# Attention with mixed heads and a mixture of experts on one core: the ten queries of a half lie 12 partitions apart in the evicted scores

## Chip, cores and metric

The kernel runs on one core of a Trainium2 chip. The metric is the time of one execution on the device in microseconds (us), as the median of several runs.

## The reference

There are B = 8 batches, H = 12 heads, S = 448 tokens, 64 numbers a head. Cut to what matters:

```python
scores = (1 / 8) * q @ k.transpose(0, 1, 3, 2)          # b h i j
scores = einsum('bhij,hg->bgij', scores, w_pre)         # heads are mixed
attn = softmax(scores, over j)
attn = einsum('bhij,hg->bgij', attn, w_post)            # heads are mixed again
x = (attn @ v).transpose(0, 2, 1, 3).reshape(3584, 768)
# eight experts; each token goes to the one with the highest gate
e = argmax(x @ w_gate); g = softmax(x @ w_gate)[e]
out = g * (relu(x @ w1[e]) @ w2[e])
```

## The kernel before

**Tiles.** A batch's 448 queries are cut into four tiles of `IT` = 120, the last with 88. A tile is `T`, 32 in all; `it = T % 4`. A tile is worked through in blocks of up to 20 queries, a block in two halves of `IB` = 10: six blocks for 120 queries, five for 88 (the last block has one half of 8). There are 184 blocks and 360 halves. `geom[T]` holds the batch, `it`, the number of queries and the sizes of the halves by block.

**One tile.**
- `qk` (L205): for each of six head pairs, scores of 120 queries against 448 keys, in three matmul passes of split numbers; two heads go to PSUM `bs`. ScalarE evicts them to `SI[T]` (L207): the partition is the query, and a partition holds all 12 heads, 12 x 448 floats side by side. There are two `si` buffers, so a tile's first eviction has to wait until the relayouts of the tile two before have read theirs.
- `relayout` (L224): one DMA on SyncE's queue for each half moves ten partitions of `SI[T]` to 120 partitions of `sb`, one for each query and head. A packet is one head's row of 1,792 bytes. `sb` has four buffers.
- `mix` (L234 to L236): a matmul with `Wpre`, which is block diagonal over queries, mixes the heads of a half into `bm`; VectorE takes the maxima (L235), ScalarE the exponential and its sum into `et` (L236).
- `weigh` (L244 to L249): reciprocals, and GpSimd scales `Wpost` with them into `wp`.
- `post` (L260): four matmuls for each half, with `et` as the stationary operand, mix the heads again and turn the rows: `bp` has keys on partitions, and (key chunk, head, query) along them. VectorE copies `bp` into `PT[T]` (L265), where the query is the last dimension.
- `av`, `rows`, `dispatch` (L280 to L345): attention times `v`, tokens and gates, and the routing table. `XD` takes the tokens.

The keys of the next batch come in by six loads `kr` (L88), which ScalarE and GpSimd split into `kh` and `kl` (L95, L96); queries by `qr` (L104), split at L113 and L114. Both loads are issued on SyncE's queue, among the relayouts.

**Order.** A table of steps says in which block each step of a tile is written: `qk` eight blocks ahead, `relayout` two blocks ahead, `post` one block behind `mix`. Each engine works in its own fixed order. SyncE issues the DMAs in that order as well; each waits for its buffer there.

**Experts.** From about 1060 us on, each expert's tokens are gathered and go through two weight matrices, again split. The weights come in by `wraw` (L359), the first of them during the last tiles of attention.

Of the kernel before, what the change touches and what calls it, by code (L numbers as in the profile page):

```python
# [19 lines left out]
B, H, S, D = 8, 12, 448, 64  # L20
# [5 lines left out]
IB = 10  # L26
NB = 2 * IB
IQ = 5
R0, R1 = 4, 124
# [11 lines left out]
def attn_moe_kernel(ctx, tc, qT, kT, v, w_pre, w_post, w_gate, w1, w2, out):  # L41
    nc = tc.nc
# [4 lines left out]
    XD = dram.tile([NT, HD], F32, name="XD")  # L47
    TB = dram.tile([ROWS, 2], F32, name="TB")

    geom = []  # L50
    for T in range(NTILE):
        it = T % 4
        ni = min(IT, S - it * IT)
        geom.append((T // 4, it, ni, [[min(IB, ni - i) for i in range(s, min(s + NB, ni), IB)]
                                      for s in range(0, ni, NB)]))


    kq = ctx.enter_context(ExitStack())
# [23 lines left out]
    KR, KK, QR, QQ, VV, SI, SB, EE, PT, XT = ({} for _ in range(10))  # L82
# [14 lines left out]
        KK[b, c] = (kh, kl)  # L97

    def load_q(T):
        b, it, ni, _ = geom[T]  # L100
        qr = q_p.tile([P, NPAIR, IT], F32, name="qr", bufs=1)
        src = qT[b, :, H * it * IT:H * (it * IT + ni)].rearrange("d (c t i) -> t d c i", c=NPAIR, t=2)
        for half in range(2):
            nc.sync.dma_start(out=qr[half * D:(half + 1) * D, :, :ni], in_=src[half])  # L104
        QR[T] = qr
# [26 lines left out]
    for c in range(NPAIR):  # L132
# [22 lines left out]
        out=Wpre[:, R0:].rearrange("p (i g) -> p i g", g=H),  # L155
# [13 lines left out]
    for c in range(NPAIR):  # L169
# [22 lines left out]
                        in_=none.unsqueeze(1).to_broadcast([P, 8, ROWS // P // 8, 2]))  # L192


    def qk(T, c):
        b, it, ni, _ = geom[T]
        if c == 0:
            SI[T] = si_p.tile([IT, H, S], F32, name="si")
        kh, kl = KK[b, c]
        qh, ql = QQ[T]  # L200

        for n, (qx, kx) in enumerate(((qh, kh), (qh, kl), (ql, kh))):
            for r in range(2):
                hs = slice(r * D, (r + 1) * D)
                nc.tensor.matmul(out=bank_s[:ni, r, :S], lhsT=qx[hs, c, :ni], rhs=kx[hs, :],  # L205
                                 start=(n == 0), stop=(n == 2))
        nc.scalar.copy(out=SI[T][:ni, 2 * c:2 * c + 2, :], in_=bank_s[:ni, :, :S])  # L207
        m = (it - 2) * NPAIR + c - NPAIR + 2
        if b + 1 < B:
            if 0 <= m < NPAIR:  # L210
                load_k(b + 1, m)
            if 1 <= m <= NPAIR:
                split_k(b + 1, m - 1)
# [5 lines left out]
    def relayout(T, s):  # L219
        sb = sbs[nsb["n"] % len(sbs)]  # L220
        nsb["n"] += 1
        for c, nq in enumerate(geom[T][3][s]):
            q0 = s * NB + c * IB
            nc.sync.dma_start(out=sb[R0:R0 + nq * H, c, :], in_=SI[T][q0:q0 + nq])  # L224
        SB[T, s] = sb

    def mix(T, s):
# [25 lines left out]
    def post(T, s):  # L253
        if s == 0:
            PT[T] = pt_p.tile([JC, NJ, H, IT], F32, name="pt")
        et, wp = EE.pop((T, s))
        for n, nq in enumerate(geom[T][3][s]):
            pp = bank_p[n]
            for c in range(NJ):
                nc.tensor.matmul(out=pp[:, c * IT:(c + 1) * IT],  # L260
                                 lhsT=et[:R1, n, c * JC:(c + 1) * JC],
                                 rhs=wp[:R1, n, :], start=True, stop=True)
        for n, nq in enumerate(geom[T][3][s]):
            i0 = s * NB + n * IB
            nc.vector.tensor_copy(  # L265
                out=PT[T][:, :, :, i0:i0 + nq].rearrange("p c h i -> p (c h) i"),
                in_=bank_p[n][:, :NJ * IT].rearrange("p (x i) -> p x i", i=IB)[:, :, :nq])

    PA = {}


    def av(T, g):
        b, it, ni, _ = geom[T]
        if g == 0:
            XT[T] = x_p.tile([P, NPAIR, IT], F32, name="xt")
        for p in range(3):
            for c in range(NJ):
                for r in range(2):
                    h = 2 * (3 * g + p) + r
                    nc.tensor.matmul(out=bank_a[r * D:(r + 1) * D, p, :ni],  # L280
                                     lhsT=VV[b][:, c, h * D:(h + 1) * D],
                                     rhs=PT[T][:, c, h, :ni], start=(c == 0), stop=(c == NJ - 1))
        nc.vector.tensor_copy(out=XT[T][:, 3 * g:3 * g + 3, :ni], in_=bank_a[:, :, :ni])  # L283
# [1 line left out]
    XR, LG = {}, {}  # L285

    def rows(T, part):
        b, it, ni, _ = geom[T]
        if part == 0:
            XR[T] = x_p.tile([IT, NPAIR, P], F32, name="xr", bufs=1)  # L290
            LG[T] = sm_p.tile([IT, 2, NE], F32, name="lg")
        px = bank_x[part] if T == NTILE - 1 else bank_x[0]
        pxv = px[:, :3 * XG].rearrange("p (c x) -> p c x", x=XG)
        for c in range(3):
            nc.tensor.matmul(out=pxv[:ni, c, :], lhsT=XT[T][:, part * 3 + c, :ni],
                             rhs=xg[:, part * 3 + c, :], start=True, stop=True)
        nc.scalar.copy(out=XR[T][:ni, part * 3:part * 3 + 3, :], in_=pxv[:ni, :, :P])
        nc.vector.reduce_sum(out=LG[T][:ni, part, :],
                             in_=pxv[:ni, :, P:XG].rearrange("p c e -> p e c"), axis=AX.X)
        if part == 1:  # L300
            t0 = b * S + it * IT
            nc.sync.dma_start(out=XD[t0:t0 + ni, :],
                              in_=XR.pop(T)[:ni].rearrange("p c x -> p (c x)"))
# [1 line left out]
    state = {"base": base0}  # L305

    def dispatch(T):
        b, it, ni, _ = geom[T]
        lg2 = LG.pop(T)
        lg = sm_p.tile([IT, NE], F32, name="lgs")  # L310
        nc.vector.tensor_add(out=lg[:ni], in0=lg2[:ni, 0, :], in1=lg2[:ni, 1, :])
        m8 = sm_p.tile([IT, NE], F32, name="m8")
        i8 = sm_p.tile([IT, NE], U32, name="i8")
        nc.vector.max(out=m8[:ni], in_=lg[:ni])
        nc.vector.max_index(out=i8[:ni], in_max=m8[:ni], in_values=lg[:ni])
        sc = sm_p.tile([IT, 4], F32, name="sc")
        nc.vector.tensor_copy(out=sc[:ni, 0:1], in_=i8[:ni, 0:1])
        ohb = sm_p.tile([IT, NE], BF16, name="ohb")
        nc.vector.tensor_scalar(out=ohb[:ni], in0=iota8[:ni], scalar1=sc[:ni, 0:1], scalar2=None,
                                op0=ALU.is_equal)  # L320
        pr = bank_x[0]
        nc.tensor.matmul(out=pr[:ni, 0:NE], lhsT=tri[:ni, :ni], rhs=ohb[:ni], start=True, stop=True)
        nc.tensor.matmul(out=pr[:, NE:2 * NE], lhsT=ones[:ni, :], rhs=ohb[:ni], start=True, stop=True)
        nc.vector.tensor_scalar(out=sc[:ni, 1:2], in0=m8[:ni, 0:1], scalar1=-1.0, scalar2=None,
                                op0=ALU.mult)
        ex = sm_p.tile([IT, NE], F32, name="ex")
        nc.scalar.activation(out=ex[:ni], in_=lg[:ni], func=AF.Exp, bias=sc[:ni, 1:2],
                             scale=1.0, accum_out=sc[:ni, 2:3])
        nc.vector.tensor_scalar(out=sc[:ni, 2:3], in0=sc[:ni, 2:3], scalar1=1e-9, scalar2=None,
                                op0=ALU.add)  # L330
        tg = sm_p.tile([IT, 2], F32, name="tg")
        nc.vector.reciprocal(out=tg[:ni, 1:2], in_=sc[:ni, 2:3])
        nc.vector.tensor_copy(out=tg[:ni, 0:1].bitcast(I32), in_=tokid[:ni, b, it:it + 1])
        pos = sm_p.tile([IT, NE], F32, name="pos")
        nc.vector.tensor_tensor(out=pos[:ni], in0=pr[:ni, 0:NE], in1=state["base"][:ni], op=ALU.add)
        nc.vector.tensor_tensor(out=pos[:ni], in0=pos[:ni], in1=ohb[:ni], op=ALU.mult)
        di = sm_p.tile([IT, 1], I32, name="di")
        nc.vector.reduce_sum(out=sc[:ni, 3:4], in_=pos[:ni], axis=AX.X)
        nc.vector.tensor_copy(out=di[:ni], in_=sc[:ni, 3:4])
        nc.gpsimd.indirect_dma_start(  # L340
            out=TB[:, :], out_offset=bass.IndirectOffsetOnAxis(ap=di[:ni, 0:1], axis=0),
            in_=tg[:ni, :], in_offset=None, bounds_check=ROWS - 1, oob_is_err=False)
        last = T == NTILE - 1
        nbase = (const if last else sm_p).tile([P, NE], F32, name="cbase" if last else "nbase")
        nc.vector.tensor_tensor(out=nbase, in0=pr[:, NE:2 * NE], in1=state["base"], op=ALU.add)  # L345
        state["base"] = nbase
# [31 lines left out]
        steps.setdefault(u, []).append(what)  # L378

    for T in range(NTILE):  # L380
        b, it, ni, _ = geom[T]
        u0, n = ustart[T], len(geom[T][3])
        if T:
            at(max(u0 - QLEAD - 4, -1), 0, load_q, T)
# [178 lines left out]
    with tc.For_i(0, nslots, 1):  # L563
# [20 lines left out]
        for n, rows in enumerate((HD, FF)):  # L584
# [9 lines left out]
            out=tb[:, :], out_offset=None, in_=TB[:, :],  # L594
# [74 lines left out]
```

## Time and profile before

| | |
|---|---|
| median of 3 runs | 1654.72 us (1654.67 to 1656.5) |
| the profiled execution | 1650.6 us |
| its span | 1648.4 us |
| mean granted clock of TensorE | 0.974 |
| DMA | 197.51 MB, mean 120 GB/s |

The profile is of one execution. PE is TensorE's matmul, PEld its weight load, DVE is VectorE, ACT ScalarE, POOL GpSimd, SP SyncE; SPq is SyncE's queue, where a row's length is the time that the issue took, not that of the transfer. In rows of groups, "out<-in" gives tile names, then the shapes (partitions x elements), the count, the busy time in us, the mean ns of one, and the idle time before it with what ended it. In square brackets of a timeline row stands the idle time of that engine just before, and what ended it.

### The profile page before, as it was taken

Reading aid. Unit: us, or ns where it says so; the run is one execution under the profiler, and the core shown is the slowest. Engines: PE = TensorE matmul, PEld = TensorE weight load, DVE = VectorE, ACT = ScalarE, POOL = GpSimd, SP = SyncE. Lnnn points to the kernel's source line nnn. Section 1 sums busy time; section 2 is a strip of 40 time slices with the busy share of each in tenths; the row PEclk is TensorE's granted clock in tenths of the full one; section 3 lists DMA queues with packets and bytes.
Section 4 is the critical chain, followed back from the end, with each engine's and each line's share of the span. In section 5 each row is a group of like instructions: output and inputs, shape, how many; then the busy total and the mean of one; then the engine's idle time right before and its main releaser. Section 6 shows DMA issues by size and latency. Waiting matters only on the chain. (4 is left out here: it accounts for less than half of the span.)

```text
span 1648.4 us, 29453 instructions
## 1 busy us (share of the span) xinstructions
PE 1528.3 (93%) x11056; PEld 1202.8 (73%) x11056; DVE 816.0 (50%) x2003; ACT 663.2 (40%) x1424; POOL 429.3 (26%) x595
## 2 busy tenths in 40 slices
PE   4798998998998998998999998859999999999996
PEld 2576776776776776776777776659888888997986
DVE  0465665564665565664666666643342433335330
ACT  3454444454454444444445443323241332224220
POOL 4243243243233333333333321222020210102000
PEclk9899999999999999999999999979999999999998
DMA  6555655565566565565555545253351624326210
GB/s 163 120 114 111 121 127 111 99 145 115 99 139 127 98 138 116 107 134 118 112 126 112 110 87 135 68 174 123 133 183 55 219 76 154 132 93 220 94 48 36
DMA packets 114465, 197.51 MB, mean 120 GB/s; under 512 B 39746, under 2 KB 88914, under 8 KB 114308
## 3 DMA queue, kind: packets, MB, share of 16 engines
q1 hardware_dynamic: 107200, 171.51, 44.7%
q0 software_dynamic: 6064, 23.86, 4.0%
q8 instruction: 100, 1.64, 0.4%
q14 instruction: 57, 0.47, 0.1%
q10 hardware_dynamic: 1044, 0.04, 0.0%
HBM read 96.01 MB, written 23.06 MB: 72 GB/s over the span
## 5 line engine op out<-in xcount | busy, mean ns | idle before, releaser
L236 ACT ACTIVATE et<-bm,st 124x448 f32<-124x448 f32 x360 | 226.2, 633 | 408.0 <-DVE st L235 325.6
L260 PEld LDWEIGHTS bp<-wp,et 124*112 124x112 f32 x2880 | 314.3, 179 | 70.2 <-issue 53.6
L249 POOL TENSOR_SCALAR wp<-Wpost,st 124x120 f32<-124x120 f32 x360 | 208.2, 590 | 602.5 <-DVE st L246 567.6
L260 PE MATMUL bp<-wp,et 124*112 124x120 f32 x2880 | 350.9, 275 | 13.7 <-POOL wp L249 8.8
L234 PE MATMUL bm<-sb,Wpre 124*124 124x448 f32 x720 | 307.9, 549 | 2.9 <-DMA sb<-si 2.9
L265 DVE COPY pt<-bp 112x480 f32<-112x480 f32 x360 | 234.3, 653 | 79.7 <-PE bp L260 78.0
L235 DVE TENSOR_REDUCE st<-bm 124x1 f32<-124x448 f32 x360 | 224.0, 623 | 47.2 <-PE bm L234 36.0
L207 ACT COPY si<-bs 120x896 f32<-120x896 f32 (+1 forms) x192 | 172.4, 898 | 66.8 <-PE bs L205 39.2
L280 PEld LDWEIGHTS ba<-pt,vt 112*64 112x64 f32 x3072 | 157.8, 141 | 33.3 <-issue 21.4
L280 PE MATMUL ba<-pt,vt 112*64 112x120 f32 (+1 forms) x3072 | 175.3, 269 | 1.2 <-DVE pt L265 0.7
L234 PEld LDWEIGHTS bm<-sb,Wpre 124*124 124x124 f32 x720 | 121.2, 189 | 73.1 <-issue 65.5
L205 PEld LDWEIGHTS bs<-kh,qh 64*120 64x120 f32 (+1 forms) x384 | 34.7, 177 | 165.3 <-issue 94.9
L525 POOL DMA_INDIRECT out<-y,ti x30 | 33.4, 1112 | 465.1 <-ACT xh L452 337.7
L497 PE MATMUL pm_h<-xh,ah 128*128 128x512 f32 (+1 forms) x384 | 147.3, 384 | 1.9 <-ACTq L549 0.8
L497 PE MATMUL pm_h<-xh,al 128*128 128x512 f32 (+1 forms) x384 | 146.9, 383 | 0.0
L497 PE MATMUL pm_h<-xl,ah 128*128 128x512 f32 (+1 forms) x384 | 146.9, 383 | 0.0
L205 PE MATMUL bs<-kh,qh 64*120 64x448 f32 (+1 forms) x384 | 92.2, 477 | 53.2 <-ACT si L207 44.4
L516 PE MATMUL pm_y<-bh,hh 128*128 128x384 f32 x480 | 127.9, 343 | 0.0
L516 PE MATMUL pm_y<-bl,hh 128*128 128x384 f32 x480 | 123.6, 336 | 0.0
L516 PE MATMUL pm_y<-bh,hl 128*128 128x384 f32 x480 | 121.0, 336 | 0.0
L501 DVE SCALAR_TENSOR_TENSOR hl<-pm_h,hh 128x512 fp32r<-128x512 f32 (+1 forms) x64 | 42.0, 657 | 139.1 <-ACT hh L500 139.1
L283 DVE COPY xt<-ba 128x360 f32<-128x360 f32 (+1 forms) x64 | 32.5, 507 | 139.0 <-PE ba L280 139.0
(102 smaller groups left out, 1746.4 us busy)
## 6 DMA issues: line engine op xcount, KB each, us to landing
sb<-si SPq DMA_DIRECT2D x352, 210.0 KB
wraw<-in_w SPq DMA_DIRECT2D x48, 512.0 KB
wraw<-in_w SPq DMA_DIRECT2D x64, 384.0 KB
kr<-in_kT SPq DMA_DIRECT2D x48, 224.0 KB
vt<-in_v SPq DMA_DIRECT2D x8, 1344.0 KB
qr<-in_qT SPq DMA_DIRECT2D x48, 180.0 KB
XD<-xr SPq DMA_DIRECT2D x24, 360.0 KB
qr<-in_qT SPq DMA_DIRECT2D x16, 132.0 KB
```

The source lines that it names most:

```text
L205: nc.tensor.matmul(out=bank_s[:ni, r, :S], lhsT=qx[hs, c, :ni], rhs=kx[hs, :], start=(n == 0), stop=(n == 2))
L207: nc.scalar.copy(out=SI[T][:ni, 2 * c:2 * c + 2, :], in_=bank_s[:ni, :, :S])
L234: nc.tensor.matmul(out=bm, lhsT=Wpre[:R1, :], rhs=sb[:R1, c, :], start=True, stop=True)
L235: nc.vector.reduce_max(out=st[:R1, 0, c:c + 1], in_=bm, axis=AX.X, negate=True)
L236: nc.scalar.activation(out=et[:R1, c, :], in_=bm, func=AF.Exp, bias=st[:R1, 0, c:c + 1], scale=1.0, accum_out=st[:R1, 1, c:c + 1])
L249: nc.gpsimd.tensor_scalar(out=wp[:R1, c, :], in0=Wpost[:R1], scalar1=st[:R1, 2, c:c + 1], scalar2=None, op0=ALU.mult)
L260: nc.tensor.matmul(out=pp[:, c * IT:(c + 1) * IT], lhsT=et[:R1, n, c * JC:(c + 1) * JC], rhs=wp[:R1, n, :], start=True, stop=True)
L265: nc.vector.tensor_copy(out=PT[T][:, :, :, i0:i0 + nq].rearrange("p c h i -> p (c h) i"), in_=bank_p[n][:, :NJ * IT].rearrange("p (x i) -> ...
L280: nc.tensor.matmul(out=bank_a[r * D:(r + 1) * D, p, :ni], lhsT=VV[b][:, c, h * D:(h + 1) * D], rhs=PT[T][:, c, h, :ni], start=(c == 0), st ...
L497: nc.tensor.matmul(out=ph[:, :n], lhsT=wx[:, fs], rhs=xx[:, kt, :n], start=(m == 0), stop=(m == 3 * NK1 - 1))
L501: nc.vector.scalar_tensor_tensor(out=hl[:, ft, :n], in0=ph[:, :n], scalar=0.0, in1=hh[:, ft, :n].bitcast(F32), op0=ALU.max, op1=ALU.subtract)
L516: nc.tensor.matmul(out=py[g][:, :384], lhsT=hx[:, kt, ts], rhs=wx[:, g * 384:(g + 1) * 384], start=(n == 0), stop=(n == 3 * NK2 - 1))
```

## The change

A half's ten queries are no longer neighbours. A tile of 120 queries has N = 12 halves, and half n takes the queries n, n + 12, n + 24 and so on. In the evicted scores they lie 12 partitions apart. The relayout DMA reads those partitions, and writes the same 120 partitions of `sb`. In `PT` the copy writes every 12th column; after it, `PT` holds what it held before, so nothing behind it changes. A tile of 88 queries has nine halves: seven of ten queries and two of nine, 9 partitions apart, where before it had eight of ten and one of eight.

```diff
-        geom.append((T // 4, it, ni, [[min(IB, ni - i) for i in range(s, min(s + NB, ni), IB)]
-                                      for s in range(0, ni, NB)]))
+        N = -(-ni // IB)
+        halves = [-(-(ni - n) // N) for n in range(N)]
+        geom.append((T // 4, it, ni, [halves[n:n + 2] for n in range(0, N, 2)], N))
+
+    def queries(T, s, c):
+        N, n = geom[T][4], 2 * s + c
+        return slice(n, n + N * (geom[T][3][s][c] - 1) + 1, N)
...
     def relayout(T, s):
...
         for c, nq in enumerate(geom[T][3][s]):
-            q0 = s * NB + c * IB
-            nc.sync.dma_start(out=sb[R0:R0 + nq * H, c, :], in_=SI[T][q0:q0 + nq])
+            nc.sync.dma_start(out=sb[R0:R0 + nq * H, c, :], in_=SI[T][queries(T, s, c)])
...
     def post(T, s):
...
         for n, nq in enumerate(geom[T][3][s]):
-            i0 = s * NB + n * IB
             nc.vector.tensor_copy(
-                out=PT[T][:, :, :, i0:i0 + nq].rearrange("p c h i -> p (c h) i"),
+                out=PT[T][:, :, :, queries(T, s, n)].rearrange("p c h i -> p (c h) i"),
                 in_=bank_p[n][:, :NJ * IT].rearrange("p (x i) -> p x i", i=IB)[:, :, :nq])
```

The order of the instructions is the same on every engine. What differs is shapes, in two places. On VectorE, in the steady state of a tile of 120 queries (`st` holds maxima and sums), before:

```order
L265 COPY pt<-bp_110 112x48x10
L265 COPY pt<-bp_111 112x48x10
L235 TENSOR_REDUCE st<-bm_108 124x1
L235 TENSOR_REDUCE st<-bm_109 124x1
L244 TENSOR_SCALAR st<-st 124x2
```

and after (the lines are seven further down):

```order
L271 COPY pt<-bp_110 112x480
L271 COPY pt<-bp_111 112x480
L242 TENSOR_REDUCE st<-bm_108 124x1
L242 TENSOR_REDUCE st<-bm_109 124x1
L251 TENSOR_SCALAR st<-st 124x2
```

The copy wrote 48 runs of ten floats; now it writes 480 floats at one constant distance, 48 bytes, as 12 steps of the query are ten to a head and 120 columns a head. On SyncE's queue, at the end of a batch's last tile, before:

```order
L224 DMA sb_180<-si 120x1x448 x2
L302 DMA XD<-xr 120x768
L224 DMA sb_181<-si 120x1x448 x2
L224 DMA sb_182<-si 96x1x448
L224 DMA sb_183<-si 120x1x448 x2
```

and after:

```order
L231 DMA sb_180<-si 120x1x448 x2
L308 DMA XD<-xr 120x768
L231 DMA sb_181<-si 120x1x448
L231 DMA sb_181<-si 108x1x448
L231 DMA sb_182<-si 108x1x448
L231 DMA sb_183<-si 120x1x448 x2
```

The transfers stand where they stood; the last two of the tile have 108 rows each, in place of 120 and 96.

More of the change, by code (lines that the diff above doesn't have):

```diff
@@ L99, in load_q @@
     def load_q(T):
-        b, it, ni, _ = geom[T]
+        b, it, ni = geom[T][:3]
         qr = q_p.tile([P, NPAIR, IT], F32, name="qr", bufs=1)
@@ L195, in qk @@
     def qk(T, c):
-        b, it, ni, _ = geom[T]
+        b, it, ni = geom[T][:3]
         if c == 0:
@@ L272, in av @@
     def av(T, g):
-        b, it, ni, _ = geom[T]
+        b, it, ni = geom[T][:3]
         if g == 0:
@@ L287, in rows @@
     def rows(T, part):
-        b, it, ni, _ = geom[T]
+        b, it, ni = geom[T][:3]
         if part == 0:
@@ L307, in dispatch @@
     def dispatch(T):
-        b, it, ni, _ = geom[T]
+        b, it, ni = geom[T][:3]
         lg2 = LG.pop(T)
@@ L380, in attn_moe_kernel @@
     for T in range(NTILE):
-        b, it, ni, _ = geom[T]
+        b, it, ni = geom[T][:3]
         u0, n = ustart[T], len(geom[T][3])
```

## Prediction

> **What bounds the kernel now.** I read the page's engine rows first, then busy time in stretches cut at the attention tiles, then the waits, then the timeline around one large wait, with SyncE's queue beside it. The page says that TensorE (PE) is busy nearly all the time, and the chain that ended last lies in the experts at the end, which the change leaves alone. So the question is what PE's idle time in the attention half is made of.
>
> ```profile
> span 1648.4 us, 29453 instructions
> PE 1528.3 (93%) x11056; PEld 1202.8 (73%) x11056; DVE 816.0 (50%) x2003; ACT 663.2 (40%) x1424; POOL 429.3 (26%) x595
> ```
>
> One call gives a table by tile: the stretches run from the first `bm` matmul of one tile to that of the next. Columns are the stretch, its length, each engine's busy time with its instructions, PE's granted clock, the share of 16 DMA engines that was busy, and GB/s.
>
> ```profile
> 32.69:74.67 41.98, 31.98 (x147) 19.70 (x147) 15.25 (x33) 16.13 (x36) 11.29 (x17) 0.89 0.57 114
> 106.85:145.18 38.33, 34.17 (x277) 24.61 (x274) 20.15 (x55) 17.73 (x42) 14.35 (x20) 0.96 0.61 125
> ...
> 233.94:273.95 40.01, 34.99 (x276) 25.27 (x274) 20.20 (x55) 17.73 (x42) 14.21 (x20) 0.91 0.58 120
> 362.73:403.36 40.63, 35.24 (x277) 25.54 (x274) 20.34 (x55) 17.73 (x42) 14.24 (x20) 0.92 0.58 121
> 492.38:530.88 38.50, 34.15 (x276) 24.61 (x274) 20.33 (x55) 17.85 (x42) 14.21 (x20) 0.96 0.60 125
> 619.64:660.15 40.51, 34.60 (x277) 25.04 (x274) 20.33 (x55) 17.74 (x42) 14.21 (x20) 0.92 0.58 118
> 748.91:789.18 40.27, 35.15 (x276) 25.45 (x274) 20.34 (x55) 17.74 (x42) 14.21 (x20) 0.92 0.59 122
> 877.95:910.92 32.97, 32.67 (x276) 23.42 (x274) 20.33 (x55) 16.81 (x40) 11.95 (x18) 1.00 0.56 112
> 999.67:1037.64 37.97, 30.96 (x250) 23.03 (x248) 21.70 (x51) 16.22 (x35) 7.44 (x13) 0.96 0.63 161
> ```
>
> Seven of these are the third tile of batches 0 to 6, with the same PE work (276 or 277 matmuls). Batch 6 does it in 32.97 us, PE busy for 32.67 of them at clock 1.00. The six before take 38.33 to 40.63, PE idle for 4 to 6 us and the clock at 0.91 to 0.96. So each of the six loses 5.4 to 7.7 us, partly as idle time, partly as slower matmuls. The first tile (41.98, of which 10.0 idle) and the third of the last batch (37.97, 7.0 idle) lose time too. The waits from 60 to 1060 us (us, times, longest) name first whom PE waits for:
>
> ```profile
> PE bs L205 <- ACT si L207: 36.3, 15, 5.9
> ```
>
> ScalarE's eviction `si` holds PE. The timeline shows one such place, and what ScalarE itself waits for; below it SyncE's own rows ahead of that place (start, us, count).
>
> ```profile
> 257.36 0.91 ACT L207 COPY si<-bs 120x896 f32<-120x896 f32 x1 [4.61 <-DMA sb<-si]
> 258.32 0.73 PE L205 MATMUL bs<-kh,qh 64*120 64x448 f32 x2 [5.02 <-ACT si L207]
> ```
>
> ```profile
> 237.01 1.70 SPq L224 DMA_DIRECT2D sb<-si  x2
> 238.80 5.58 SPq L88 DMA_DIRECT2D kr<-in_kT  x2
> 244.47 1.69 SPq L224 DMA_DIRECT2D sb<-si  x2
> 246.25 2.56 SPq L88 DMA_DIRECT2D kr<-in_kT  x1
> 248.91 2.09 SPq L224 DMA_DIRECT2D sb<-si  x2
> ```
>
> The eviction may not overwrite an `si` buffer until the relayouts (L224) have read it. The last pair was issued from 248.91 to 251.00 and was still under way at 257.3. And SyncE issues without a pause: a `kr` load holds it for 2.6 to 2.8 us. At the start, with the queue empty, the same issue took 0.34, and the first relayout, issued at 27.02, released PE at 32.69:
>
> ```profile
> 19.97 0.34 SPq L88 DMA_DIRECT2D kr<-in_kT  x1
> ...
> 27.02 7.50 SPq L224 DMA_DIRECT2D sb<-si  x4
> ...
> 32.69 1.83 PE L234 MATMUL bm<-sb,Wpre 124*124 124x448 f32 x2 [1.69 <-DMA sb<-si]
> ...
> 35.53 1.85 PE L234 MATMUL bm<-sb,Wpre 124*124 124x448 f32 x2 [1.01 <-DMA sb<-si]
> ```
>
> So PE's large waits hang on how long a relayout takes and on a queue that its transfers fill.
>
> **The change: the relayout's read side.** The 352 relayouts stay, with the same bytes; only the ten source partitions change. How slow is the read now? The first two rows are stretches in which nearly all traffic is relayout, and then weight loads of the experts; the third is the queue's row for the first stretch (packets, MB, share).
>
> ```profile
> 28.00:34.00 6.00, 3.31 (x12) 1.28 (x8) 0.00 (x0) 1.81 (x2) 0.00 (x0) 1.00 0.52 88
> ...
> 1200.00:1400.00 200.00, 194.87 (x998) 173.31 (x997) 77.36 (x103) 64.88 (x99) 29.05 (x24) 1.00 0.40 142
> ```
>
> ```profile
> q1 hardware_dynamic: 314, 0.53, 51.6%
> ```
>
> ```profile
> sb<-si SPq DMA_DIRECT2D x352, 210.0 KB
> TB<-none POOLq DMA_DIRECT2D x1, 224.0 KB, 3.4
> ```
>
> 314 packets took 0.516 x 16 x 6.0 = 49.5 us of engine time: 158 ns for one of 1.7 KB, or 10.7 GB/s for an engine. The weight loads run at 142 / (0.40 x 16) = 22.2 GB/s an engine; at that rate a packet of 1.79 KB (215,040 bytes in 120 packets) takes 81 ns. Some eight engines were busy, so a relayout occupies them for 120 x 158 / 8.3 = 2.3 us now and 1.2 at the other rate: it would land 1.1 us sooner at least. From above: its 5.67 us (27.02 to 32.69) could fall to the 3.4 us in which `TB<-none`, of the same size, landed: 2.3 us. Below nothing would be a relayout that gets slower; the rows give no reason, since the bytes, the count and the written side stay. I take 2.3, because ten neighbours that hinder each other explain the missing half of the rate, and behind a pair of relayouts the queue saves more: a load issued into a free queue costs 0.34 instead of 2.6. In the stretch quoted above three `kr` loads hold SyncE for 8.14 us, against 1.0. So the last pair can go out some 5 us sooner where no wait of its own holds it, and lands 2.3 sooner still: more than the 4.61 us that ScalarE waited.
>
> [...]
>
> **What this is worth, by tile.** The six third tiles: 38.33 + 40.01 + 40.63 + 38.50 + 40.51 + 40.27 = 238.3; at batch 6's 32.97 they make 197.8; gain 40.4. It takes in the lower clock after each wait. The first tile: of its 10.0 us of idle time 9. The wait of 1.69 at its start: 1.7. The last batch's third tile, where ScalarE waits for loads of expert weights behind the same queue: 7.0 idle; these loads are larger, so I take 4. Sum: 55.1.
>
> **The change: the copy into `pt` (L265).** The matrix multiplies see the same sizes, since a column of `pt` is a query as before. The copy now writes single floats 48 bytes apart, not runs of ten. Its neighbours:
>
> ```profile
> L265 DVE COPY pt<-bp 112x480 f32<-112x480 f32 x360 | 234.3, 653 | 79.7 <-PE bp L260 78.0
> ...
> L283 DVE COPY xt<-ba 128x360 f32<-128x360 f32 (+1 forms) x64 | 32.5, 507 | 139.0 <-PE ba L280 139.0
> ...
> L298 DVE TENSOR_REDUCE lg<-bx 120x8 f32<-120x24 f32 (+1 forms) x63 | 11.4, 182 | 36.4 <-ACT xr L297 36.4
> ...
> L338 DVE TENSOR_REDUCE sc<-pos 120x1 f32<-120x8 f32 (+1 forms) x32 | 4.8, 148 | 0.0
> ```
>
> No row has such a write. L283 writes whole rows: 120 elements more make L265 146 ns longer, 1.2 ns each. L298 reads 24 floats 544 bytes apart, 34 ns above L338 with 8 in a row: 2.1 ns each. So the copy costs between 632 ns (no runs to start: 480 x 1.04 + 132) and 653 + 480 x 0.9 = 1085. I take an unchanged 653, as two small reductions are thin evidence, and keep both ends. [...]
>
> What hides it, in one block (two halves) of the steady state:
>
> ```profile
> 500.23 1.15 POOL L249 TENSOR_SCALAR wp<-Wpost,st 124x120 f32<-124x120 f32 x2 [1.22 <-DVE st L246]
> 502.67 0.66 DVE L265 COPY pt<-bp 112x480 f32<-112x480 f32 x1 [0.46 <-PE bp L260]
> 503.49 0.66 DVE L265 COPY pt<-bp 112x480 f32<-112x480 f32 x1 [0.16 <-PE bp L260]
> 504.31 1.31 DVE L235 TENSOR_REDUCE st<-bm 124x1 f32<-124x448 f32 x2 [0.17 <-PE bm L234]
> 505.66 0.63 ACT L236 ACTIVATE et<-bm,st 124x448 f32<-124x448 f32 x1
> 505.66 1.89 PE L260 MATMUL bp<-wp,et 124*112 124x120 f32 x16
> 508.09 1.67 PE L234 MATMUL bm<-sb,Wpre 124*124 124x448 f32 x4
> ```
>
> Two copies of 1.09 us would end at 502.67 + 2.18 = 504.85, so the maximum (L235) starts 0.54 us late, and the exponential that waits for it ends at 506.83 in place of 506.29. The next `bm` comes at 508.09: 1.3 us are left. The next `bp` needs the copies' bank at 505.66 (0.8 left) and weights made by 501.4. So PE waits in few blocks. With that cover gone it would be 0.54 us for each of 184 blocks, 99 us. I charge 1 us.
>
> **The change: the last tile of a batch.** Its 88 queries make seven halves of ten and two of nine, not eight of ten and one of eight: the same bytes and number of instructions. Nothing.
>
> **Sum.** 1650.6 (the profiled execution; its span is 1648.4) - 55.1 + 1 = 1596.5. The median of the runs is 4.1 above the profiled execution, so I say 1600.
>
> **Rivals.**
> 1. *The waits only shrink.* The relayout gains its lower end, 1.1 us, and one `kr` load's 2.2: 3.3 of each 5.0. For it: the lower bound rests on measured rates alone. Gain 6 x 3.3 + half of the other 14.7 = 27: 1628. Chance 0.12.
> 2. *No change.* Buffers hide the relayouts, and `bm` itself hardly ever waits for them (1.69 + 1.01 us at the start). Against it: the wait in the timeline is on the source buffer, not on `sb`. 1654. Chance 0.03.
> 3. *Slower.* The strided copy is so slow that PE waits for VectorE in every block: behind L235 stands the exponential, and then `bm`. [...] It decides from 55 / 184 = 0.30 us a block. Against it: the slack of 1.3 us above, which two copies use up only from about 1.7 us each. Chance 0.06.
> [...]
>
> **Numbers.** The forecast (1586 to 1618, with 4 in it) has 0.79. The range reaches to rival 1: 1586 to 1632. Below 1586 there is no idle time of this kind left. Within 0.2% (3.3 us, about what a measurement of this kernel can tell from no change) lies rival 2. Faster 0.91, same 0.03, slower 0.06.
>
> **What would show it.** In the profile after: the six third tiles near 33 us at clock 1.00; no wait of `si` for `sb<-si`; `kr` issues near 0.34; a DMA share well under 0.58 at no fewer GB/s; L265's new mean, and whether PE waits for VectorE. I am wrong if packets keep their 158 ns, if another buffer takes over the wait, or if the maxima (L235) start late and `bm` with them.

## The result, and the profile after

The changed kernel takes 1591.03 us (median, 1589.22 to 1594.46) against 1654.7: a ratio of 0.9616, 95% interval 0.9595 to 0.9637. The prediction said 1600, with a range of 1586 to 1632. The profiled execution took 1589.22 us, with a span of 1587.0. Run again later, the ratio was 0.961 (0.958 to 0.9639).

From the page: the span, PE's and VectorE's busy time, and SyncE's queue (packets, MB, share of 16 engines), which stood at 44.7% before for the same packets.

```profile
span 1587.0 us, 29453 instructions
...
PE 1511.4 (95%) x11056; PEld 1190.4 (75%) x11056; DVE 892.5 (56%) x2003; ACT 661.5 (42%) x1424; POOL 429.8 (27%) x595
...
q1 hardware_dynamic: 107200, 171.51, 33.4%
```

The table by tile, as before: the first tile, the third tiles of two of the six batches that lost time, of batch 6, and of the last batch.

```profile
30.70:57.68 26.98, 26.56 (x148) 16.53 (x147) 16.89 (x33) 17.01 (x37) 10.58 (x16) 1.00 0.63 200
89.44:122.42 32.98, 32.68 (x277) 23.43 (x274) 22.59 (x56) 17.51 (x42) 14.35 (x20) 1.00 0.48 138
211.21:244.22 33.01, 32.71 (x276) 23.41 (x274) 22.61 (x56) 17.51 (x42) 14.19 (x20) 1.00 0.45 138
...
820.41:853.39 32.98, 32.68 (x277) 23.43 (x274) 22.61 (x56) 16.68 (x40) 11.99 (x18) 1.00 0.31 104
942.18:973.41 31.23, 29.16 (x251) 21.37 (x248) 24.08 (x51) 16.04 (x34) 7.45 (x13) 1.00 0.57 186
```

All third tiles of batches 0 to 6 now take 32.97 to 33.01 us, PE is busy for all but 0.3 of it, and the clock is at 1.00 throughout. In the six tiles that had lost time DMA moves 138 GB/s at a share of 0.45 to 0.48, against some 120 at 0.58 to 0.61: 138 / (0.46 x 16) = 19 GB/s for a busy engine, where it was 13.

The waits from 60 to 1060 us, PE's and the eviction's:

```profile
ACT si L215 <- PE bs L213: 24.5, 29, 1.0
...
PE bs L213 <- ACT si L215: 4.4, 14, 0.6
PE bp L267 <- POOL wp L256: 3.9, 3, 1.8
```

After 60 us the eviction no longer waits for a DMA in any place; PE's 36.3 us behind it are 4.4. SyncE's rows in the third tile of batch 1, and the eviction that had waited 4.61 us:

```profile
218.31 1.68 SPq L231 DMA_DIRECT2D sb<-si  x2
221.85 0.34 SPq L96 DMA_DIRECT2D kr<-in_kT  x1
226.05 1.68 SPq L231 DMA_DIRECT2D sb<-si  x2
...
229.92 0.90 ACT L215 COPY si<-bs 120x896 f32<-120x896 f32 x1
```

A `kr` issue takes 0.34 us where it took 2.6 to 2.8, SyncE stands idle between issues, and the eviction starts without a wait (no bracket). The first relayouts, from the queue's row for 28 to 32 us:

```profile
q1 hardware_dynamic: 545, 0.87, 59.4%
```

545 packets took 0.594 x 16 x 4.0 = 38.0 us of engine time: 70 ns each (65 of them are short ones of the query loads), where 314 had taken 158 ns.

What the change costs is in VectorE's copy, 653 ns before:

```profile
L271 DVE COPY pt<-bp 112x480 f32<-112x480 f32 x360 | 344.3, 1011 | 47.8 <-PE bp L267 47.1
```

### The profile page after: what moved, and what is told of

Its sections match the earlier page's. It is cut to its first block, busy times and chain, and to the rows that moved or that the text cites. A ratio compares the mean times of both kernels' runs of the same rounds, so it can differ in the third digit from the quotient of the medians.

```text
span 1587.0 us, 29453 instructions
## 1 busy us (share of the span) xinstructions
PE 1511.4 (95%) x11056; PEld 1190.4 (75%) x11056; DVE 892.5 (56%) x2003; ACT 661.5 (42%) x1424; POOL 429.8 (27%) x595
## 5 line engine op out<-in xcount | busy, mean ns | idle before, releaser
L271 DVE COPY pt<-bp 112x480 f32<-112x480 f32 x360 | 344.3, 1011 | 47.8 <-PE bp L267 47.1
L267 PEld LDWEIGHTS bp<-wp,et 124*112 124x112 f32 x2880 | 309.5, 177 | 60.3 <-issue 51.8
L267 PE MATMUL bp<-wp,et 124*112 124x120 f32 x2880 | 345.8, 272 | 4.6 <-POOL wp L256 3.9
L242 DVE TENSOR_REDUCE st<-bm 124x1 f32<-124x448 f32 x360 | 218.4, 614 | 25.1 <-PE bm L241 17.1
L286 PEld LDWEIGHTS ba<-pt,vt 112*64 112x64 f32 x3072 | 151.7, 138 | 32.3 <-issue 22.1
L286 PE MATMUL ba<-pt,vt 112*64 112x120 f32 (+1 forms) x3072 | 169.0, 263 | 1.5 <-DVE m L320 1.0
L527 DVE TENSOR_SCALAR y<-pm_y,tb 128x384 f32<-128x384 f32 x30 | 18.4, 614 | 159.9 <-PE pm_y L522 159.9
```

Source lines behind the costliest of these rows:

```text
L242: nc.vector.reduce_max(out=st[:R1, 0, c:c + 1], in_=bm, axis=AX.X, negate=True)
L267: nc.tensor.matmul(out=pp[:, c * IT:(c + 1) * IT], lhsT=et[:R1, n, c * JC:(c + 1) * JC], rhs=wp[:R1, n, :], start=True, stop=True)
L271: nc.vector.tensor_copy(out=PT[T][:, :, :, queries(T, s, n)].rearrange("p c h i -> p (c h) i"), in_=bank_p[n][:, :NJ * IT].rearrange("p (x ...
L286: nc.tensor.matmul(out=bank_a[r * D:(r + 1) * D, p, :ni], lhsT=VV[b][:, c, h * D:(h + 1) * D], rhs=PT[T][:, c, h, :ni], start=(c == 0), st ...
```

## Experiments

### One half of the change at a time

**Reads 12 apart, copy in runs.** The queries are laid out in the input so that partition n + 12 k of a tile holds query 10 n + k; the output is the same.

```diff
...
-                out=PT[T][:, :, :, queries(T, s, n)].rearrange("p c h i -> p (c h) i"),
+                out=PT[T][:, :, :, columns(T, s, n)].rearrange("p c h i -> p (c h) i"),
...
-            inputs["q"][:, :, i:i + IT].transpose(0, 3, 1, 2).reshape(B, D, -1)
+            inputs["q"][:, :, i + _spread(min(IT, S - i))].transpose(0, 3, 1, 2).reshape(B, D, -1)
```

> The ten partitions of a half stay 12 apart, but the copy into pt writes runs of ten floats again; the queries are laid out in another order in the input, so that nothing else changes. Theory (the gain is the relayout's read alone, and the slower copy is hidden): 1591 us, within 4 us of the changed kernel; DMA queue q1 at 33% of 16 engines; L271's mean back at 653 ns; third tiles at 33.0 us. Rival (the slower copy costs PE time, some 0.03 to 0.1 us in each of 184 blocks): 1575 to 1586 us.

Measured: 1584.82 us, ratio 0.9576 (0.9552 to 0.96). The page's queue and copy:

```profile
q1 hardware_dynamic: 107200, 171.51, 33.6%
...
L275 DVE COPY pt<-bp 112x480 f32<-112x480 f32 x360 | 234.4, 653 | 74.6 <-PE bp L271 72.9
```

The whole gain is there without the strided copy. The time is 6.2 us under the changed kernel, outside the 4 us that the theory allowed and in the rival's range: the copy seemed to cost some 6 us. Tiles in the middle do not show it: a first tile of a later batch takes 29.80 us here and 29.85 with the strided copy. To price the copy, both kernels were run on one chip.

> The changed kernel as it is, on one chip with the next run, to price its strided copy. Theory (the copy is hidden but for the end of attention, where it costs some 3.4 us, and the first tile): 3 to 7 us above the next run, at a ratio to before of 0.960 to 0.964. Rival (the difference of 6 us between the earlier jobs came from the chips): within 2 us of the next run.

> Reads 12 apart, copy in runs of ten, beside the changed kernel on one chip. Theory: ratio to before 0.956 to 0.959, first weights of the experts 57.7 us after the last tile's start against 61.1 in the changed kernel. Rival: the ratios agree within 0.001.

Measured: 1591.49 us (ratio 0.961, 0.958 to 0.9639) and 1588.14 (0.9586, 0.9557 to 0.9615). The difference is 3.35 us this time, and the intervals overlap. The place that the theory named held in the first pair of profiles and not in the second: from the last tile's start to the first `pm_h` matmul it was 61.1 us with the strided copy and 57.7 with runs, and then 58.5 and 58.7. What differs there is PE's clock: its mean is 0.78 over the 61.1 us, and 0.81 over the 57.7 and the 58.5. In all four, PE waits for VectorE near the last copies, for 0.7 to 1.0 us:

```profile
1000.78 1.00 PE L286 MATMUL ba<-pt,vt 112*64 112x88 f32 x14 [1.01 <-DVE m L320]
...
1001.93 2.90 PE L286 MATMUL ba<-pt,vt 112*64 112x88 f32 x34
```

```profile
998.61 0.82 PE L290 MATMUL ba<-pt,vt 112*64 112x88 f32 x14 [0.70 <-DVE pt L275]
...
999.59 1.58 PE L290 MATMUL ba<-pt,vt 112*64 112x88 f32 x34
```

The first two rows are of the first run of the changed kernel, where the 34 matmuls behind the wait took 2.90 us; the others are of reads 12 apart with a copy in runs (1.58, as in the second run of the changed kernel). The second run of the changed kernel has the same wait of 1.01 us at this place, and the same 34 matmuls took 1.58 us behind it. So 2.6 of the 3.4 us that the expectation put down to the copy (61.1 against 58.5) lie between two runs of the same kernel, one in which the clock fell behind this wait (to 0.50, from 1001.28 to 1004.69 us) and one in which the matmuls kept their pace. The profiles as a whole show no cost either. The last tile starts at 973.4 and 972.6 us with the strided copy, and at 972.4 and 972.9 with runs; from there to the end it takes 613.6 and 609.1 us, and 608.2 and 615.7. The medians differ by 3 to 6 us, and the intervals allow between nothing and some 10: whether the copy costs anything, and where, stays open. Reads 12 apart with a copy in runs has the lowest medians of all kernels here, but it is not clearly apart from the changed one.

**Reads side by side, copy strided.** The mirror image: partition 10 n + k holds query n + 12 k.

```diff
...
-            nc.sync.dma_start(out=sb[R0:R0 + nq * H, c, :], in_=SI[T][queries(T, s, c)])
+            nc.sync.dma_start(out=sb[R0:R0 + nq * H, c, :], in_=SI[T][columns(T, s, c)])
...
```

> The other half of the change alone: ten partitions side by side, the copy into pt writes floats 48 bytes apart. Theory: the copy takes 1011 ns in the mean as in the changed kernel, q1 is back at 45%, the third tiles with kr loads take 38 to 41 us, and the time is that of before plus 0 to 10 us: 1654 to 1665 us. Rival (the copy, or its place in VectorE's queue, has a part in the gain): below 1645 us.

Measured: 1658.03 us, ratio 1.0005 (0.9981 to 1.003). Three of the third tiles:

```profile
104.27:143.98 39.71, 35.15 (x276) 25.46 (x274) 22.62 (x56) 17.71 (x42) 14.37 (x20) 0.91 0.59 121
232.78:271.38 38.60, 34.20 (x277) 24.65 (x274) 22.61 (x56) 17.71 (x42) 14.21 (x20) 0.96 0.58 121
360.19:401.14 40.95, 34.16 (x277) 24.60 (x274) 22.70 (x56) 17.81 (x42) 14.26 (x20) 0.92 0.58 115
```

q1 was at 44.6% and the copy at 1011 ns. The copy brings nothing, and the waits are all back.

### How far apart

**Two and four apart.** Halves take every second query of 20, or every fourth of 40; what is left of a tile stays side by side. The halves of a tile have the sizes that they had before the change.

```diff
...
-        N, n = geom[T][4], 2 * s + c
-        return slice(n, n + N * (geom[T][3][s][c] - 1) + 1, N)
+        n, nq, far = 2 * s + c, geom[T][3][s][c], 2     # or 4
+        if (n // far + 1) * far * IB > geom[T][2]:
+            return slice(n * IB, n * IB + nq)
+        first = n // far * far * IB + n % far
+        return slice(first, first + far * (IB - 1) + 1, far)
```

> Ten partitions 2 apart (a half spans 20), copy 8 bytes apart. [...] Rival (only the mean packet counts, and that hardly falls): third tiles at 38 or more, above 1640 us. Rival 2 (any distance over 1 frees the reads): q1 at 33%.

> Ten partitions 4 apart (a half spans 40), copy 16 bytes apart. [...]

Measured: 1598.27 us (0.9651, 0.9625 to 0.9676), inside my estimate of 1592 to 1610, and 1596.84 (0.9636, 0.961 to 0.9662), 0.8 us above my estimate of 1589 to 1596. Queue and copy of the pages, two apart and then four:

```profile
q1 hardware_dynamic: 107200, 171.51, 41.8%
...
L273 DVE COPY pt<-bp 112x480 f32<-112x480 f32 x360 | 234.6, 653 | 76.9 <-PE bp L269 75.2
```

```profile
q1 hardware_dynamic: 107200, 171.51, 36.1%
...
L273 DVE COPY pt<-bp 112x480 f32<-112x480 f32 x360 | 351.2, 1032 | 51.2 <-PE bp L269 50.4
```

The queue's time is share x 16 x span. If all that differs is put down to the 43,008 packets of the relayouts, a packet costs over that of the changed kernel: side by side (0.447 x 16 x 1648.4 - 0.334 x 16 x 1587.0) / 43,008 = 77 ns more, two apart 50 ns, four apart 17 ns. So in these four kernels a packet costs less the farther apart the partitions lie. By what means neighbours slow each other was not shown.

Four apart can tell within one kernel whether distance is all that counts. Its halves in partitions 0 to 39 and those in 40 to 79 have the same distance, and the last eight queries of a batch lie side by side. These are the queue's rows while two transfers of the first kind are under way (354 to 358 us), two of the second (364 to 368.3), and then the eight neighbours (373 to 377):

```profile
q1 hardware_dynamic: 241, 0.40, 33.9%
```

```profile
q1 hardware_dynamic: 260, 0.43, 26.3%
```

```profile
q1 hardware_dynamic: 78, 0.14, 32.0%
```

That is 0.339 x 16 x 4.0 / 241 = 90 ns a packet, 70 and 263. Halves with the same distance differ, 90 ns against 70, so distance alone does not explain it; what sets them apart was not shown. With eight neighbours, and no other transfer in the queue, a packet takes nearly four times the 70 ns.

Two apart moves the mean packet by only a third of the way, and yet the third tiles are at 32.98 to 33.00 us and the gain is nearly whole. This is one of them:

```profile
216.89:249.87 32.98, 32.69 (x276) 23.43 (x274) 20.34 (x55) 17.52 (x42) 14.13 (x20) 1.00 0.59 137
```

The DMA engines are as busy in it as in the kernel before (0.59, where it was 0.58 to 0.61), and three of its four `kr` issues take 0.34 to 0.35 us, the fourth 1.8. So the third tiles do not hang on the mean load. What fell is the slow end: of the packets of 1,792 bytes (relayouts and `kr` loads) in the two traces, 28% took over 200 ns in the kernel before, and 3% two apart. Whether it is the slowest packets of a transfer that the buffer waits for was not shown apart. The first tile still waits (32.5 us against 27.0): ScalarE stands there for 5.2 us until a `kr` load has landed.

### Where the time was lost

**Third tiles only.** Every other tile reads side by side, in halves as before the change.

```diff
...
-        N, n = geom[T][4], 2 * s + c
-        return slice(n, n + N * (geom[T][3][s][c] - 1) + 1, N)
+        n, nq = 2 * s + c, geom[T][3][s][c]
+        if geom[T][1] != 2:
+            return slice(n * IB, n * IB + nq)
+        return slice(n, n + 12 * (nq - 1) + 1, 12)
```

> Only the third tile of each batch (88 of the 352 relayouts and a quarter of the copies) takes its queries 12 apart; all other tiles as before. Theory (the lost time sits where the third tile's last relayouts hold the si buffer): the six third tiles that took 38 to 41 us take 33.0 to 33.5, the last batch's third tile some 33 to 35, the first tile stays at 40 to 42; 1607 to 1615 us, so a quarter of the edit brings two thirds of the gain. Rival (a gain spread over all relayouts, through the load on the DMA engines): a quarter of the gain, 1638 us.

Measured: 1613.49 us, ratio 0.9736 (0.9702 to 0.977). The first tile, two third tiles, the last batch's third tile:

```profile
32.35:76.38 44.03, 32.07 (x147) 19.94 (x147) 15.27 (x33) 16.24 (x36) 11.27 (x17) 0.90 0.56 111
108.94:141.93 32.99, 32.70 (x277) 23.42 (x274) 22.18 (x55) 17.51 (x42) 14.32 (x20) 1.00 0.53 114
230.68:263.69 33.01, 32.71 (x276) 23.41 (x274) 22.18 (x55) 17.52 (x42) 14.18 (x20) 1.00 0.47 113
961.46:998.86 37.40, 32.16 (x250) 23.91 (x248) 23.91 (x50) 16.11 (x35) 7.43 (x13) 0.91 0.53 148
```

A quarter of the relayouts (96 of 360; the 352 in the expectation are those of 120 rows) frees all six third tiles, and two thirds of the gain with them. The first tile was 2 us over the range given, and I was wrong on the last batch: its third tile stays at 37.40, so its waits (ScalarE stands for 11.2 us until expert weights have landed, against 12.2 before) hang on other tiles' relayouts in the queue too.

**The same slow reads, asked for later.** The kernel before, with scores written seven blocks ahead.

```diff
-    PL, QLEAD, RLEAD = 1, 8, 2
+    PL, QLEAD, RLEAD = 1, 7, 2
```

> The kernel before, its reads side by side, but every tile's scores are written seven blocks ahead in place of eight, so that the eviction asks for the si buffer one block (about 5 us) later. The order on all engines shifts with that. Theory (a wait for a buffer that comes free late): the six third tiles fall from 38 to 41 us to 33 to 35, DMA share and q1 stay at 45%; 1608 to 1635 us. Rival (slow transfers hold PE wherever one asks for them): third tiles still above 37 us, 1645 us or more.

Measured: 1631.09 us, ratio 0.983 (0.9786 to 0.9873), q1 at 45.1%. ScalarE's waits for DMAs from 60 to 1000 us in the kernel before:

```profile
ACT kh L95 <- DMA kr<-in_kT: 33.2, 13, 8.0
...
ACT si L207 <- DMA kr<-in_kT: 14.2, 3, 5.5
ACT si L207 <- DMA sb<-si: 13.3, 3, 5.0
```

and in this one, with PE's wait for ScalarE:

```profile
ACT kh L95 <- DMA kr<-in_kT: 61.7, 13, 9.7
...
PE bm L234 <- ACT et L236: 15.7, 6, 5.1
...
ACT si L207 <- DMA sb<-si: 3.5, 3, 1.6
...
ACT si L207 <- DMA kr<-in_kT: 1.7, 1, 1.7
```

The six waits of the evictions, 27.5 us, are the six third tiles. In three of them the profile names a `kr` load as what ended the wait. The eviction reads no `kr`, but relayouts and `kr` loads share one queue, so these three rows do not tell by themselves that the buffer was what held it. Asked for one block later, the buffer is nearly always free: 5.2 us are left, and the six third tiles fall to 34.1 to 37.6 us. This speaks for the `si` buffer. But two of the six stay above 37 (I had said 33 to 35), since ScalarE waits longer for `kr` loads that still stand behind slow relayouts, 61.7 us where it was 33.2, and PE waits for ScalarE. The shift also costs time elsewhere: the third tile of batch 6, which had lost none, goes from 32.97 to 36.80 us. The later request brings 1.7% where the faster read brings 3.8%. Both the buffer and the queue are part of the cause; as the shift moves the order on every engine, the run does not tell their shares.

### How much slower the copy may become

**Copy in runs, twice; strided copy, twice.**

```diff
-            nc.vector.tensor_copy(
+            for _ in range(2):
+              nc.vector.tensor_copy(
...
```

> Reads 12 apart, the copy in runs of ten made twice: 1.31 us of VectorE for each half. By the slack read from the timeline (two copies of up to 1.7 us each stay hidden), the middle tiles keep their 29.8, 31.8 and 33.0 us, and only the uncovered end of attention grows, by 4 to 7 us: 1588 to 1594 us. Rival (the slack of one block does not hold where tokens are routed as well): 1600 to 1620 us, tiles 1 to 2 us longer.

> The changed kernel with its strided copy made twice: 2.02 us of VectorE for each half, over the 1.7 us of the slack. VectorE's busy time in a tile of six blocks would be 19.5 + 12 x 1.37 = 35.9 us against 29.8 of PE: VectorE becomes the bound, tiles of 120 take 36 to 38 us, those of 88 some 28 to 30, 1710 to 1750 us in all. Rival (the slack is longer than read, since the copy may fall behind by a block): below 1650 us.

Measured: 1609.35 us (0.9722, 0.9686 to 0.9759) and 1770.35 (1.0684, 1.0647 to 1.0721). A first tile and a third tile of each, runs and then strided:

```profile
152.84:182.79 29.95, 29.89 (x263) 21.15 (x261) 24.18 (x73) 15.60 (x39) 8.78 (x14) 1.00 0.52 161
214.55:248.79 34.24, 32.79 (x276) 23.47 (x274) 26.12 (x68) 17.60 (x43) 14.34 (x20) 1.00 0.44 132
```

```profile
174.75:207.76 33.01, 30.44 (x263) 21.29 (x261) 29.57 (x73) 15.16 (x37) 8.34 (x14) 1.00 0.48 147
243.46:284.48 41.02, 35.54 (x276) 25.18 (x274) 32.62 (x67) 17.30 (x42) 14.26 (x19) 0.96 0.37 114
```

The first time is in the rival's range (1600 to 1620), not in the 1588 to 1594 of the theory. At 1.3 us a half the third tile takes 1.25 us more, and the end of attention, up to the first `pm_h`, 6.5 to 7.5 us more. In the third tile VectorE is busy for only 26 of 34 us, so it is not full; PE waits there in two places, 0.9 us for the last copies before `ba` and 0.6 for an eviction. At 2.0 us a half all tiles are slowed, and the kernel is slower than before the change, by 20 us more than the upper end that I had put. The third tiles suffer most (41 us, where 36 to 38 was expected), the first tiles of later batches less (33), and the tiles of 88 queries take 33.8, where 28 to 30 was expected. VectorE is not full in the two tiles shown either (29.6 of 33.0 us, 32.6 of 41.0).

## Why the prediction was right

**The main mechanism held, to a tenth.** The six third tiles were to give 40.4 us, and gave 238.25 - 197.92 = 40.3. That the read side is the cause is shown (a packet took 158 ns side by side, and 70 at 12 apart): spreading the reads alone brings the gain, the strided copy alone brings none, and third tiles alone bring two thirds. The wait on `si` and the full queue are both shown to take part, but the prediction read the buffer from one place of six; of the other five, three name a `kr` load. The 352 relayouts of the prediction are those of 120 rows; there are 360. Rival 2 (no change) fell; rival 1 (waits that only shrink) fell for the third tiles.

**Two terms were too small.** The first tile with its start was charged at 9 + 1.7 and gave 15.0 + 2.0. I had counted its idle time alone; PE's busy time there fell as well, from 31.98 to 26.56 us, as the clock went from 0.89 to 1.00. In the kernel before, ScalarE stood in this tile for 5.6 us until a `qr` load had landed and for 8.0 until a `kr` load had; both waits are gone, so much of this term lies with the queue. For the six third tiles this was in the sum, since they were compared with one that had no wait. Behind the wait of 5.02 us the clock stood at 0.50 from 258.32 to 263.30 us, and each of the six waits of 4 to 6 us left its tile at 0.91 to 0.96. But a single wait of that length is not needed: in the first run of the changed kernel the clock stood at 0.50 from 1001.28 to 1004.69 us, behind the wait of 1.01 us. The last batch's third tile was charged at 4 and gave 6.7, again with its clock (0.96 to 1.00); the second run of the changed kernel has 31.92 us there, so 6.0.

**One term was wrong in its value, and little hung on it.** I took an unchanged 653 ns for the strided copy, against two reductions that spoke for 1085. It is 1011, close under the upper end. I had set aside the only rows that had a bearing. The 1.04 ns a float in the lower end is what L283 shows in the kernel before, 532 ns for 360 floats and 432 for 264; the 507 is the mean of both shapes. That the time hardly moved is due to the slack, not to this value. In kind it is a slow copy that stays hidden, which the forecast counts in as 4. The 1 us charged for the copy is neither borne out nor refuted: the medians say 3 to 6 us, and the profiles show none. The slack of 1.7 us read from one block was too long as well: 1.3 us is already seen.

**The sum.** Tiles: 40.3 + 15.0 + 2.0 + 6.7 = 64.0 us; the other tiles keep their times within 0.5 us. From the last tile's start to the end it took 610.8 us before and 613.6 after, 2.8 more, but a second profile of the changed kernel has 609.1 there, so this is no more than runs differ by. Together that makes, to within 0.3 us, the 61.4 by which the span fell. The 1596.5 us that the prediction had for the profiled execution were 7.3 too many: it gave the tiles some 9 us too little and the copy 1 us that does not show, and the end came out 2.8 longer.

## What to carry to other kernels

A wait for a buffer that a DMA still reads can show up as an engine waiting for an eviction, as PE did here for 5.02 us behind `si`; follow it to the transfer, and then look at the issuing queue: here a `kr` issue took 2.6 us while slow relayouts stood in the queue, and 0.34 once they were faster. Which partitions a transfer reads from can matter as much as its bytes: with partitions side by side a packet of an SBUF-to-SBUF transfer took 158 ns here, where it took 70 with partitions 12 apart, and even two apart was enough to take the waits of the third tiles away (32.98 to 33.00 us). Price a wait by a stretch that does the same work without it, as the slower clock behind it (0.91 to 0.96 in the six third tiles, 1.00 without the wait) is then counted too.

## What the runs showed of the hardware

- **A strided write of VectorE.** 480 floats from PSUM took 653 ns with runs of ten, 653 with floats 8 bytes apart, 1032 at 16 and 1011 at 48 (means over all copies; those of the tiles of 88 queries differ a little in size and distance). So the step lies between 8 and 16 bytes, costs 0.75 to 0.79 ns a float, and did not grow up to 48.
- **A relayout's packet** of 1,792 bytes costs 77 ns more when its ten source partitions are side by side than when they are 12 apart, 50 when two apart and 17 when four apart, as means over a run, worked out from the queue's shares. Alone in the queue, with eight source partitions side by side, it took 263 ns, and 70 with ten four apart in partitions 40 to 79.
- **The granted clock** went to 0.50 for 3.4 us behind a wait of 1.01 us in one run of the changed kernel, where the next 34 matmuls took 2.90 us; behind the same wait in another run they took 1.58.
